# Layer 3 of a four-layer kernel in one pass: each weight part serves both pairs of batches, two block products are added up in PSUM, GpSimd's subtractions go to VectorE

## The chip, the core and the metric

The kernel runs on one core of a Trainium2 chip. The metric is device time in microseconds (us) from launch to end, as the median of several runs; one further execution was profiled. In the profile PE is TensorE's matmul row and PEld its weight loads, DVE is VectorE, ACT ScalarE, POOL GpSimd and SP SyncE, which here issues nearly all DMAs.

## The reference, cut to what matters

```python
scores = cap * tanh((q @ k.T / sqrt(64)) / cap)          # 4 batches, 12 heads, 448 x 64
x   = softmax(scores) @ v                                 # -> 1792 tokens x 768
h   = max(x @ w1, x @ w2, x @ w3)                         # layer 1, 768 x 768 each
y   = h @ w_out                                           # layer 2, 768 x 768
u   = sigmoid(y @ w_gate) * (y @ w_val)                   # layer 3, 768 x 1536 each
out = u @ moe2_w_out                                      # layer 4, 1536 x 768
```

The weights come as 64-bit floats; an fp32 copy is decoded on the chip.

## The kernel before, in words

Every product in fp32 is made of three matmul passes: each operand is split into a high part (an fp32r copy, on ACT) and a low part (operand minus high part), and high·high, high·low and low·high are added up in PSUM. A matmul takes 128 x 128 weights and 448 columns (one batch's tokens).

The stages follow each other in one program: attention and layer 1 are interleaved up to about 400 us; then the rest of layer 1, layer 2, layer 3 and layer 4. The order in which the instructions of one engine stand is made by a scheduler from the order of the code; each engine then works strictly in that order.

**Weights.** `raw_bits` (L51) loads 64-bit words by DMA into a buffer called `wraw`, `decode` (L57) turns them into fp32 with one ACT and four DVE instructions, and `decode_ahead` (L71) does this for the weights of later layers and stores the result in DRAM (`ws`), from where the layers load them again. It is stepped from the loops of layers 1 to 3.

**Layer 3** works with two batches and two column blocks at a time as a 2 x 2 block product in seven products instead of eight (the form of Strassen and Winograd). The text calls one such group a *quad*: column block pair j (0 to 5), gate (m = 0) or value (m = 1) weights, and one pair of batches. Its products are numbered 1, 2, 6, 7, 5, 4, 3; each is nine matmuls. Per quad, `Layer3.prepare` (L425) makes four sums of weight blocks on DVE (L434 to L437) and then, for each product, one weight *part*: a high copy on ACT (L444) and a low one by a subtraction (L445), which for products 1, 2, 4, 7 and 3 is on POOL and for 5 and 6 on DVE. The parts lie in a *ring* of nine slots; the code works four parts ahead (`AHEAD = 4`).

`after` (L468) adds the products up in SBUF (`temps`), seven DVE additions per quad, each with one operand in PSUM. For gate quads a sigmoid on ACT follows (L494), for value quads a multiplication with the gate (L496) and a DMA of the result to DRAM (`us`, L497).

There are two *passes*: 12 quads with the pair of batches (1, 2), then 12 with the pair (3, 0), each loading, summing and splitting all weights anew. So layer 3 has 24 quads, 168 products and 1512 matmuls. The input parts of the second pair are made inside layer 3 by hooks: `build` (L820) splits three chunks each, and five of these seven builds stand in the last quad of the first pass (`half`, L833).

**Layer 4** (L499) is of the same seven-product kind. `form` (L514) makes its weight sums in layer 3's second pass; `first_side` (L527) gives its first weights the `wraw` and `wf` buffers, 1 quad before the end; `fetch` (L509) loads the layer 3 results, `split` (L554) splits them.

Of the kernel before, what the change touches and what calls it, by code (L numbers as in the profile page):

```python
# [17 lines left out]
def tile_kernel(ctx: ExitStack, tc: tile.TileContext, q, k, v, cap, w1, w2, w3, wo, wg, wv, wo2, out):  # L18
# [31 lines left out]

    def raw_bits(wpool, src, shape):  # L51
        raw = wpool.tile([*shape, 2], I32, tag="wraw", name="wraw", bufs=2)
# [14 lines left out]
    def widths(wpool, src, shape):  # L67
        raw = raw_bits(wpool, src, shape)
        return decode(wpool.tile(shape, F32, tag="wf", name="wf", bufs=2), raw)

    def decode_ahead(wpool, items, place):  # L71

        raw, done = None, None
        for src, shape, keep in (*items, (None,) * 3, (None,) * 3):
# [4 lines left out]
            if raw is not None:  # L79
                if place[0] == "s":  # L80
                    t = wpool.tile([P, 3, HC, P], F32, tag="s", name="wd", bufs=1)
                    t = t.rearrange("p a c f -> p (a c f)")[:, :DM]
                else:
                    t = wpool.tile([P, DM], F32, tag="wf", name="wd", bufs=2)
                if len(raw[1]) == 3:
                    t = t.rearrange("p (c f) -> p c f", c=KC)
                done = decode(t, raw[0]), raw[2]
# [10 lines left out]
    def col_block(wpool, w, j, keep=None, kept=False, sub=None):  # L98
        shape = [P, KC, P]
        if kept:  # L100
            wf = wpool.tile(shape, F32, tag="wf", name="wf", bufs=2)
# [285 lines left out]
    def layer2_plain(h2, y2, mm, wpool):  # L387
        wt = col_block(wpool, wo, 0, wso[0], True)
        for j in range(KC):
            this = wt  # L390
            if j + 1 < KC:
                wt = col_block(wpool, wo, j + 1, wso[j + 1], True)
            for h, y in zip(h2, y2):
                ps = mm.tile([P, 512], F32, tag="mm", name="mm")
                product(ps[:, :S], this, h)
                nc.scalar.copy(y[:, j], ps[:, :S])
            yield

    class Layer3:

        AHEAD = 4

        def __init__(self, passes, rooms, mm, wpool, hooks):
            self.passes, self.rooms, self.mm, self.wpool, self.hooks = passes, rooms, mm, wpool, hooks
            self.quads = [(n, j, m) for n in range(len(passes)) for j in range(NF // 2) for m in range(2)]
            self.seq = [(k, i) for k in range(len(self.quads)) for i in (1, 2, 6, 7, 5, 4, 3)]
            self.ready, self.wf, self.sums, self.parts = 0, {}, {}, {}

        def start(self, ring):
            self.ring = [self.rooms.flat(n, "ring") for n in ring]
            self.load(0)
            self.prepare()

        def load(self, k):
            if k < len(self.quads):
                n, j, m = self.quads[k]
# [6 lines left out]
        def prepare(self, upto=AHEAD):  # L425

            while self.ready < min(upto, len(self.seq)):
# [13 lines left out]
                r = self.ready % 9  # L441
                w = self.ring[r // 3][:, (r % 3) * 2 * HC * P : (r % 3 + 1) * 2 * HC * P]
                w = w.rearrange("p (a c f) -> p a c f", a=2, c=HC)
                nc.scalar.copy(w[:, 0], src)  # L444
                (nc.gpsimd if i in (1, 2, 4, 7, 3) else nc.vector).tensor_sub(w[:, 1], src, f(w[:, 0]))  # L445
# [3 lines left out]
        def run(self, temps):  # L449
            self.temps = temps  # L450
            for n, (k, i) in enumerate(self.seq):
                self.prepare(n + 1 + self.AHEAD)
                ps = self.mm.tile([P, 512], F32, tag="mm", name="mm")[:, :S]
                w, x = self.parts.pop((k, i)), self.passes[self.quads[k][0]][1][i]
                order = [(0, m, c) for c in range(HC) for m in range(2)] + [(1, 0, c) for c in range(HC)]
                for q, (wm, xm, c) in enumerate(order):
                    nc.tensor.matmul(  # L457
                        ps, w[:, wm, c, :], x[:, xm, c, :], start=(q == 0), stop=(q == len(order) - 1)
                    )
                self.after(k, i, ps)  # L460
# [3 lines left out]
        def temp(self, k, i):  # L464
            n = (4 * k + i) % 12
            return self.temps[n // KC][:, n % KC]

        def after(self, k, i, ps):  # L468
            c11, c12, c21, c22 = (self.temp(k, e) for e in range(4))
            add = nc.vector.tensor_add  # L470
            if i == 1:
                nc.scalar.copy(c12, ps)
            elif i == 2:
                add(c11, ps, c12)  # L474
                self.out(k, 0, c11)
            elif i == 6:
                add(c12, ps, c12)
            elif i == 7:
                add(c21, ps, c12)
            elif i == 5:  # L480
                add(c12, ps, c12)
                add(c22, ps, c21)
                self.out(k, 3, c22)
            elif i == 4:
                add(c21, ps, c21)
                self.out(k, 2, c21)
            elif i == 3:
                add(c12, ps, c12)
                self.out(k, 1, c12)

        def out(self, k, i, t):
            n, j, m = self.quads[k]
            if m == 0:
                nc.scalar.activation(t, t, AF.Sigmoid)  # L494
            else:
                nc.vector.tensor_mul(t, t, self.temp(k - 1, i))  # L496
                nc.sync.dma_start(out=us[self.passes[n][0][i % 2], 2 * j + i // 2], in_=t)  # L497

    class Layer4:  # L499
# [3 lines left out]
        FORMED = {6: 1, 7: 2, 5: 0, 4: 3}  # L503
# [10 lines left out]
        def form(self, c):  # L514
# [417 lines left out]
```

## Time and profile before

| | us |
|---|---|
| median of three runs | 1060.69 (1057.83 to 1065.54) |
| the profiled execution | 1060.79 |
| its span, first to last instruction | 1059.0 |
| PE busy, sum over the span | 1019.8 |
| DVE busy | 813.5 |
| POOL busy | 188.3 |

PE's row is nearly full over the whole span, because matmuls overlap in it; whether PE loses time is seen where it sat idle and in how many matmuls a stretch holds. DVE, ACT and POOL matter where PE waits for them.

### The profile page before, as it was taken

To read this page: it belongs to the slowest core of one execution; us is meant where nothing else is said; L and a number is where in the kernel's file an instruction comes from. 1 tells how busy PE (TensorE), PEld (TensorE's weight loads), DVE (VectorE), ACT (ScalarE), POOL (GpSimd) and SP (SyncE) were. 2 spreads that over 40 slices of the span, in tenths; PEclk is the share of its full clock that TensorE was granted. 3 is DMA by queue.
4 is the path that set the end of the run, shared out by engine and by line. 5 is a ranking of instruction groups with operands and counts; after the bars stand their busy time and mean duration, and the time that the engine had idled before them with its cause. 6 is when DMAs were issued, how large, how long until landed. Compare 5 with 4: busy or idle time off the path is not lost. (4 is left out here: it accounts for less than half of the span.)

```text
span 1059.0 us, 14671 instructions
## 1 busy us (share of the span) xinstructions
PE 1019.8 (96%) x5197; PEld 848.5 (80%) x5197; DVE 813.5 (77%) x1198; ACT 532.3 (50%) x795; POOL 188.3 (18%) x167
## 2 busy tenths in 40 slices
PE   8989999999999999999999999999699999999997
PEld 4436776777676768999998987788599999999997
DVE  4888699878788786774318999998989866995651
ACT  6886577675775754444435433435434333523230
POOL 1000000000000000004524544353444441000000
PEclk9999999999999999999999999999899999999999
DMA  6767467665665448775126347656874324631232
GB/s 181 259 212 249 139 205 242 223 207 174 224 197 172 150 165 313 243 249 195 59 75 224 109 168 242 205 179 215 277 253 152 118 70 144 211 98 45 83 105 63
DMA packets 95074, 187.84 MB, mean 177 GB/s; under 512 B 33424, under 2 KB 60944, under 8 KB 94480
## 3 DMA queue, kind: packets, MB, share of 16 engines
q1 hardware_dynamic: 94560, 186.48, 53.2%
q8 instruction: 43, 0.70, 0.3%
q10 hardware_dynamic: 432, 0.33, 0.1%
q14 instruction: 39, 0.32, 0.1%
HBM read 139.20 MB, written 47.58 MB: 176 GB/s over the span
## 5 line engine op out<-in xcount | busy, mean ns | idle before, releaser
L457 PE MATMUL mm<-part,ring 128*128 128x448 f32 x1512 | 314.8, 369 | 18.0 <-DVE ring L445 8.6
L457 PEld LDWEIGHTS mm<-part,ring 128*128 128x128 f32 x1512 | 283.3, 189 | 49.3 <-issue 9.6
L141 PE MATMUL mm<-x,wh 128*128 128x448 f32 x864 | 191.9, 371 | 2.6 <-ACT hm L342 1.2
L141 PEld LDWEIGHTS mm<-x,wh 128*128 128x128 f32 x864 | 159.7, 188 | 30.1 <-issue 5.9
L445 POOL TENSOR_TENSOR ring<-w,ring 128x384 fp32r<-128x384 f32 x96 | 120.6, 1264 | 167.6 <-ACT ring L444 144.0
L94 ACT CAST wh<-wf 128x768 fp32r<-128x768 f32 x84 | 69.9, 832 | 102.4 <-DMA wf<-ws 68.6
L95 POOL TENSOR_TENSOR wl<-wf,wh 128x768 fp32r<-128x768 f32 x12 | 23.1, 1923 | 513.4 <-ACT wh L94 493.3
L141 PE MATMUL mm<-x,wl 128*128 128x448 f32 x432 | 100.8, 369 | 0.6 <-DVE wl L95 0.5
L268 ACT ACTIVATE e<-e,capb 128x896 f32<-128x896 f32 (+1 forms) x96 | 88.9, 948 | 1.0
L141 PEld LDWEIGHTS mm<-x,wl 128*128 128x128 f32 x432 | 80.4, 188 | 9.8 <-DVE wl L95 3.0
L574 PE MATMUL mm<-w2a,u 128*128 128x384 f32 x504 | 88.0, 334 | 0.0
L574 PEld LDWEIGHTS mm<-w2a,u 128*128 128x128 f32 x504 | 87.4, 188 | 0.0
L95 DVE TENSOR_TENSOR wl<-wf,wh 128x768 fp32r<-128x768 f32 x72 | 68.6, 953 | 12.0 <-ACT wh L94 11.5
L260 ACT ACTIVATE e<-sc,tsc 128x896 f32<-128x896 f32 (+1 forms) x78 | 73.9, 968 | 4.4 <-PE sc L255 4.4
L494 ACT ACTIVATE temps<-temps 128x448 f32<-128x448 f32 x48 | 27.8, 580 | 80.5 <-DVE temps L474 32.3
L574 PE MATMUL mm<-w2b,u 128*128 128x384 f32 x378 | 66.0, 334 | 0.0
L574 PEld LDWEIGHTS mm<-w2b,u 128*128 128x128 f32 x378 | 65.6, 188 | 0.0
L288 PE MATMUL pv<-e,vs 128*64 128x448 f32 x288 | 61.3, 548 | 3.1 <-DVE r L308 3.1
L141 PE MATMUL mm<-h,wh 128*128 128x448 f32 x288 | 63.4, 369 | 0.0
L444 ACT CAST ring<-s 128x384 fp32r<-128x384 f32 x72 | 36.6, 508 | 52.5 <-DVE s L435 33.2
L444 ACT CAST ring<-w 128x384 fp32r<-128x384 f32 x96 | 48.1, 510 | 28.3 <-PE mm L457 18.9
L558 ACT CAST u<-u 128x1344 fp32r<-128x1344 f32 x24 | 31.6, 1322 | 57.9 <-PE mm L574 53.8
(136 smaller groups left out, 1448.8 us busy)
## 6 DMA issues: line engine op xcount, KB each, us to landing
wf<-ws SPq DMA_DIRECT2D x64, 384.0 KB, 3.7
w<-ws SPq DMA_DIRECT2D x48, 384.0 KB, 3.4
wraw<-in_moe_w_dram SPq DMA_DIRECT2D x18, 768.0 KB, 4.8
wraw<-in_moe_w_out_dram SPq DMA_DIRECT2D x18, 768.0 KB, 5.3
ws<-wd SPq DMA_DIRECT2D x36, 384.0 KB, 2.7
us<-temps SPq DMA_DIRECT2D x48, 224.0 KB, 2.0
u<-us SPq DMA_DIRECT2D x8, 1344.0 KB, 7.4
wraw<-in_moe_w_gate_dram SPq DMA_DIRECT2D x12, 768.0 KB, 5.6
```

The costliest lines, as they stand in the source:

```text
L94: nc.scalar.copy(wh, wf)
L95: (sub or nc.gpsimd.tensor_sub)(wl, wf, f(wh))
L141: nc.tensor.matmul(ps, a[:, c, :], at(x, m, c), start=(n == 0), stop=(n == len(passes) - 1))
L260: nc.scalar.activation(e, sc[:, :w, :S], AF.Tanh, scale=tsc)
L268: nc.scalar.activation(e, e, AF.Exp, scale=1.0 if self.general else capb)
L288: nc.tensor.matmul(self.pv[0][own, :S], lhs, e, start=(c == 0), stop=(c is None))
L444: nc.scalar.copy(w[:, 0], src)
L445: (nc.gpsimd if i in (1, 2, 4, 7, 3) else nc.vector).tensor_sub(w[:, 1], src, f(w[:, 0]))
L457: nc.tensor.matmul(ps, w[:, wm, c, :], x[:, xm, c, :], start=(q == 0), stop=(q == len(order) - 1))
L494: nc.scalar.activation(t, t, AF.Sigmoid)
L558: nc.scalar.copy(high, src[:, own])
L574: nc.tensor.matmul(ps, a, ww[g][:, w], start=(c == 0 and m == 0), stop=(c == KC - 1 and m == 2))
```

## The change

It is in layer 3 and around it.

- There is one pass. Quads are (j, m) with a list of pairs: j = 5 for the first pair (two quads), then j = 0 to 4 for both pairs (ten quads), then j = 5 for the second pair (two). Each weight part serves the first pair's product and then the second's. Parts to make: 14 quads x 7 = 98, before 168; matmuls: 1512 as before.
- The products come in the order 1, 6, 7, 2, 5, 4, 3. Product 2 is added onto product 1's bank in PSUM and product 3 onto product 5's, so five additions per quad and pair remain of seven.
- All the low parts are made on DVE; POOL has nothing to do in layer 3. The ring has three slots in the `wraw` and `wf` buffers, and `AHEAD` is 2.
- Layer 2 for the second pair (`layer2_second`) makes parts 1, 2 and 5 of that pair at once; parts 6, 7, 3 and 4 are built in the two first quads.
- All gate and value weights are decoded before layer 3 (one item every second step of layer 1's rest, before every third). Layer 4's weights are decoded and summed in layer 3 by `last_weights`, through a single `wraw` buffer, in place.
- `first_side` takes the ring's third slot for the last third of layer 4's first low weights, in the last quad, after product 5.

```diff
-    def layer2_plain(h2, y2, mm, wpool):
+    def layer2_second(h2, parts, y3, y0, t2, mm, wpool):
...
+            pa, pb = (mm.tile([P, 512], F32, tag="mm", name="mm")[:, :S] for _ in range(2))
+            product(pa, this, h2[0])
+            split(parts[1 if j < HC else 2], c, pa)
+            product(pb, this, h2[1])
+            if j < HC:
+                nc.scalar.copy(y0[:, j], pb)
+                nc.vector.tensor_sub(y3[:, j], y0[:, j], pa)
+                split(parts[5], c, y3[:, j])
...
     class Layer3:
-        AHEAD = 4
+        AHEAD = 2
+        ORDER = (1, 6, 7, 2, 5, 4, 3)
+        ONTO = {2: 1, 3: 5}
...
+            end = NF // 2 - 1
+            self.quads = [(end, m, (0,)) for m in range(2)]
+            self.quads += [(j, m, (0, 1)) for j in range(end) for m in range(2)]
+            self.quads += [(end, m, (1,)) for m in range(2)]
...
+            raw = one_of(self.wpool, "wraw", 1, [P, 2 * size], F32R, "ring")
+            self.ring = [raw[:, :size], raw[:, size:], one_of(self.wpool, "wf", 1, [P, size], F32R, "ring")]
...
                 nc.scalar.copy(w[:, 0], src)
-                (nc.gpsimd if i in (1, 2, 4, 7, 3) else nc.vector).tensor_sub(w[:, 1], src, f(w[:, 0]))
+                nc.vector.tensor_sub(w[:, 1], src, f(w[:, 0]))
...
+                for p in self.quads[k][2]:
+                    onto = self.ONTO.get(i)
+                    if onto:
+                        ps = self.open.pop((p, onto))
+                    else:
+                        ps = self.mm.tile([P, 512], F32, tag="mm", name="mm")[:, :S]
+                    if i in self.ONTO.values():
+                        self.open[p, i] = ps
...
         def first_side(self):
+            raw = one_of(self.wpool, "wraw", 0, [P, 2 * DM], F32R, "w2a")
+            high = [block(raw[:, :DM]), block(raw[:, DM:]), block(one_of(self.wpool, "wf", 0, [P, DM], F32R, "w2a"))]
+            low = [block(self.wpool.tile([P, DM], F32R, tag=tag, name="w2a", bufs=2)) for tag in ("wh", "wl")]
+            self.sides[0] = [high, low + [block(one_of(self.wpool, "wf", 1, [P, DM], F32R, "w2a"))]]
...
-            for j in range(NF):
+            for j in (*range(NF - 2, NF), *range(NF - 2)):
                 later_weights += [(cols(w, j), [P, KC, P], ws3[m, j]) for m, w in enumerate((wg, wv))]
-            later_weights += [(wo2[j * P : (j + 1) * P, :], [P, DM], ws2[j]) for j in range(NF)]
...
-            if i % 3 == 0:
+            if i % 2 == 0:
                 next(ahead)
...
+        def last_weights():
+            for c in range(KC):
+                for r in (c, KC + c):
+                    raw = raw_bits(wpool, wo2[r * P : (r + 1) * P, :], [P, DM])
+                    yield
+                    wf = decode(two(wpool, "wf", [P, DM], F32, "wd"), raw)
+                    nc.sync.dma_start(out=ws2[r], in_=wf)
+                    yield
+                t = l4.load_sums(c)
+                yield
+                l4.form(c, t)
+                yield
...
+            ((0, 1), lambda: build(6, t2, 8)),
+            ((0, 5), lambda: build(7, y0[:, tops], 9)),
+            ((1, 1), lambda: build(3, y0[:, ends], 7)),
+            ((1, 5), lambda: [build(4, y3[:, ends], 1), l3.free.extend(temps(0))]),
+            *(((k, i), step) for k in range(2, end - 1) for i in (1, 7, 5, 3)),
...
+            ((end, 7), lambda: l4.fetch("11", 1, 8)),
+            ((end, 2), lambda: l4.fetch("21", 1, 9)),
+            ((end, 5), lambda: [l4.first_side(), l4.weights(0)]),
```

How the scheduler orders it follows in rows of the built programs: line, operation, result<-operands, size, and how often in a row. The lines of the changed kernel have other numbers: `ring` L465 was L445, the sums L456 to L459 were L434 to L437, the additions are L506 to L520, the layer 3 matmuls L485, those of layer 4 L618.

First place: DVE in the middle of layer 3 while weights of layer 4 are decoded (`wd`). Before, a stretch of the first pass:

```order
L474 TENSOR_TENSOR temps<-mm,temps 128x448
L61 TENSOR_SCALAR wd<-wd 128x768
L62 TENSOR_SCALAR wd<-wd 128x768
L63 SCALAR_TENSOR_TENSOR wd<-wraw,wd 128x768
L477 TENSOR_TENSOR temps<-mm,temps 128x448
L445 TENSOR_TENSOR ring<-s,ring 128x384
L479 TENSOR_TENSOR temps<-mm,temps 128x448
L64 SCALAR_TENSOR_TENSOR wd<-wraw,wd 128x768
```

Now, in a quad that serves both pairs:

```order
L465 TENSOR_TENSOR ring<-s,ring 128x384
L456 TENSOR_TENSOR s<-w_5428 128x384
L457 TENSOR_TENSOR s<-s,w_5426 128x384
L458 TENSOR_TENSOR w_5428<-w_5426,w_5428 128x384
L514 TENSOR_TENSOR temps<-mm,temps 128x448
L459 TENSOR_TENSOR s<-w_5426,s 128x384
L72 TENSOR_SCALAR wd<-wd 128x768
L514 TENSOR_TENSOR temps<-mm,temps 128x448
L465 TENSOR_TENSOR ring<-w_5426,ring 128x384
L73 TENSOR_SCALAR wd<-wd 128x768
```

The ring's subtractions of the blocks `w` now stand on DVE between the two pairs' additions (L514 twice) and the decoding; before, they stood on POOL. POOL's own list has no L465.

Second place: SP's list in the same part of layer 3. Before:

```order
L497 DMA us<-temps 128x448 x3
L422 DMA w_5617<-ws_58 128x768
L76 DMA ws_61<-wd 128x768
L54 DMA wraw<-in_moe_w_out_dram 128x1536
L422 DMA w_5619<-ws_58 128x768
L422 DMA w_5736<-ws_58 128x768
```

Now:

```order
L65 DMA wraw<-in_moe2_w_out_dram 128x1536
L444 DMA w_6010<-ws_58 128x768
L884 DMA ws_61<-wd 128x768
L556 DMA formed<-ws_61 128x768 x2
L565 DMA wt_62<-formed 128x1536
L65 DMA wraw<-in_moe2_w_out_dram 128x1536
L444 DMA w_6209<-ws_58 128x768
```

The load of a raw slice (`wraw`) now stands right behind the store of the weight sums (`wt`) that leaves the same buffer, and the weight loads of the next quad (`w`) stand behind it.

Third place: TensorE at the hand-over from layer 3 to layer 4. Before:

```order
L141 MATMUL mm<-h,wh 128x448 x12
L141 MATMUL mm<-h,wl 128x448 x6
L457 MATMUL mm<-part,ring 128x448 x1512
L574 MATMUL mm<-w2a,u_7930 128x384 x2
L574 MATMUL mm<-w2a,u_7931 128x384
```

Now:

```order
L147 MATMUL mm<-h,wl 128x448 x6
L485 MATMUL mm<-part,ring 128x448 x1503
L618 MATMUL mm<-w2a,u_7503 128x384
L485 MATMUL mm<-part,ring 128x448 x9
L618 MATMUL mm<-w2a,u_7503 128x384
L618 MATMUL mm<-w2a,u_7504 128x384
```

And DVE's list there, now (`w2a` is layer 4's first weights, its last row the third of them that uses the ring's slot):

```order
L531 TENSOR_TENSOR temps<-mm,temps 128x448
L465 TENSOR_TENSOR ring<-s,ring 128x384
L608 TENSOR_TENSOR u<-u 128x1344
L514 TENSOR_TENSOR temps<-mm,temps 128x448
L608 TENSOR_TENSOR u<-u 128x1344
L531 TENSOR_TENSOR temps<-temps 128x448
L517 TENSOR_TENSOR temps<-mm,temps 128x448
L520 TENSOR_TENSOR temps<-mm,temps 128x448
L531 TENSOR_TENSOR temps<-temps 128x448 x2
L603 TENSOR_TENSOR u_7504<-u,u_7503 128x3x448
L603 TENSOR_TENSOR u_7579<-u,u_7578 128x3x448
L593 TENSOR_TENSOR w2a<-w2a 128x768
```

One matmul of layer 4 now stands ahead of layer 3's last product; and DVE reaches the last third of layer 4's first low weights behind eleven other rows, among them the two splits of `u` (L603).

## Rows read from the trace of the kernel before

**Rows 1.** The page: busy time of each engine, and the span in 40 slices.
```profile
PE 1019.8 (96%) x5197; PEld 848.5 (80%) x5197; DVE 813.5 (77%) x1198; ACT 532.3 (50%) x795; POOL 188.3 (18%) x167
...
DVE  4888699878788786774318999998989866995651
```

**Rows 2.** The chain that ended last: start us, us, what.
```profile
752.72 146.61 PE mm L457 x714
899.33 152.90 PE mm L574 x882
```

**Rows 3.** Stretches of layer 3: busy time of each engine, clock, DMA.
```profile
core 0: us, PE busy (x) PEld busy (x) DVE busy (x) ACT busy (x) POOL busy (x), PEclk, DMA share, GB/s
...
581.50:619.80 38.30, 38.30 (x191) 35.54 (x190) 38.30 (x57) 17.13 (x35) 21.45 (x16) 1.00 0.36 119
619.80:734.10 114.30, 107.19 (x505) 92.81 (x504) 107.31 (x166) 41.53 (x86) 50.00 (x40) 1.00 0.60 201
734.10:758.70 24.60, 15.27 (x64) 12.98 (x63) 24.60 (x38) 13.14 (x29) 11.86 (x9) 0.79 0.79 257
758.70:899.20 140.50, 140.50 (x695) 130.31 (x695) 114.06 (x180) 55.19 (x108) 55.93 (x50) 1.00 0.47 159
```

**Rows 4.** Groups, 566 to 900 us: busy us, mean ns | idle before, releasers.
```profile
L457 PE MATMUL mm<-part,ring 128*128 128x448 f32 x1512 | 314.8, 369 | 18.0 <-DVE ring L445 8.6 <-DVE temps L479 3.1 <-DVE temps L477 2.1
...
L445 POOL TENSOR_TENSOR ring<-w,ring 128x384 fp32r<-128x384 f32 x96 | 120.6, 1264 | 167.6 <-ACT ring L444 144.0 <-PE mm L457 21.2 <-DVE ring L445 2.4
...
L445 DVE TENSOR_TENSOR ring<-s,ring 128x384 fp32r<-128x384 f32 x48 | 37.0, 775 | 3.8 <-ACT ring L444 3.8
...
L474 DVE TENSOR_TENSOR temps<-mm,temps 128x448 f32<-128x448 f32 x24 | 14.7, 614 | 5.4 <-PE mm L457 4.3 <-ACT ring L444 1.0
...
L64 DVE SCALAR_TENSOR_TENSOR wd<-wraw,wd 128x768 int32<-128x768 int32 x11 | 13.7, 1247 | 0.0
...
L62 DVE TENSOR_SCALAR wd<-wd 128x768 int32<-128x768 int32 x10 | 6.0, 613 | 0.1
...
L559 DVE TENSOR_TENSOR u<-u,u 128x1344 fp32r<-128x1344 f32 x2 | 3.1, 1548 | 0.0
L549 DVE TENSOR_TENSOR w2a<-w2a 128x768 fp32r<-128x768 f32 x3 | 2.8, 948 | 1.2 <-ACT w2a L548 1.2
```

**Rows 5.** PE in order of time at the end of layer 2.
```profile
562.85 2.64 PE L141 MATMUL mm<-h,wh 128*128 128x448 f32 x12
565.33 1.40 PE L141 MATMUL mm<-h,wl 128*128 128x448 f32 x6
```

**Rows 6.** In order of time: DVE and POOL at the end of the first pass.
```profile
743.07 3.79 DVE L132 TENSOR_TENSOR part<-y,part 128x448 fp32r<-128x448 f32 x3
743.65 2.73 POOL L445 TENSOR_TENSOR ring<-w,ring 128x384 fp32r<-128x384 f32 x2
...
752.12 0.54 DVE L445 TENSOR_TENSOR ring<-s,ring 128x384 fp32r<-128x384 f32 x1
```

**Rows 7.** A stretch behind the longest wait of PE, columns as in rows 3.
```profile
752.70:756.30 3.60, 3.58 (x10) 3.20 (x11) 3.60 (x7) 2.45 (x5) 1.52 (x2) 0.50 0.94 350
```

**Rows 8.** DMAs by kind: issues, KB each, median us to landing.
```profile
wraw<-in_moe_w_out_dram SPq DMA_DIRECT2D x18, 768.0 KB, 5.3
...
us<-temps SPq DMA_DIRECT2D x48, 224.0 KB, 2.0
u<-us SPq DMA_DIRECT2D x8, 1344.0 KB, 7.4
...
wt<-formed SPq DMA_DIRECT2D x6, 768.0 KB, 4.9
...
w2a<-ws SPq DMA_DIRECT2D x6, 384.0 KB, 3.9
```

**Rows 9.** A stretch of layer 1's rest, columns as in rows 3.
```profile
400.00:425.00 25.00, 25.00 (x121) 22.45 (x120) 17.75 (x28) 9.18 (x13) 0.00 (x0) 1.00 0.85 310
```

**Rows 10.** In order of time: a wait of PE's weight loads there (in brackets).
```profile
421.39 2.36 PEld L141 LDWEIGHTS mm<-x,wh 128*128 128x128 f32 x12 [0.34 <-ACT wh L94]
```

More of the change, by code (lines that the diff above doesn't have):

```diff
@@ L48, in f, with one_of, two @@
         return ap.bitcast(F32)
+    turn, single = {}, [False]
+    def one_of(wpool, tag, n, shape, dt, name):
+        return wpool.tile(shape, dt, tag=f"{tag}{n}", name=name, bufs=1)
+    def two(wpool, tag, shape, dt, name):
+        n = 0
+        if not single[0]:
+            n = turn[tag] = 1 - turn.get(tag, 1)
+        return one_of(wpool, tag, n, shape, dt, name)
     def raw_bits(wpool, src, shape):
-        raw = wpool.tile([*shape, 2], I32, tag="wraw", name="wraw", bufs=2)
+        raw = two(wpool, "wraw", [*shape, 2], I32, "wraw")
         dims = "p c f t -> p c (f t)" if len(shape) == 3 else "p f t -> p (f t)"
@@ L446, in prepare, with run @@
                 self.parts[k, i] = w
                 self.ready += 1
-        def run(self, temps):
-            self.temps = temps
+        def run(self, free):
+            self.free = free
+            order = [(0, m, c) for c in range(HC) for m in range(2)] + [(1, 0, c) for c in range(HC)]
             for n, (k, i) in enumerate(self.seq):
                 self.prepare(n + 1 + self.AHEAD)
[L453 to L460, printed above, removed]
+                w = self.parts.pop((k, i))
+                for p in self.quads[k][2]:
+                    onto = self.ONTO.get(i)
+                    if onto:
+                        ps = self.open.pop((p, onto))
+                    else:
+                        ps = self.mm.tile([P, 512], F32, tag="mm", name="mm")[:, :S]
+                    if i in self.ONTO.values():
+                        self.open[p, i] = ps
+                    x = self.xs[p][i]
+                    for q, (wm, xm, c) in enumerate(order):
+                        nc.tensor.matmul(
+                            ps,
+                            w[:, wm, c, :],
+                            x[:, xm, c, :],
+                            start=(q == 0 and not onto),
+                            stop=(q == len(order) - 1),
+                            skip_group_check=bool(onto),
+                        )
+                    self.after(k, p, i, ps)
@@ L461, in run, with new @@
                 for hook in self.hooks.get((k, i), ()):
                     hook()
[L464 to L470, printed above, removed]
-            if i == 1:
-                nc.scalar.copy(c12, ps)
-            elif i == 2:
[L474 to L479, printed above, removed]
+        def new(self):
+            return self.free.pop(0)
```

206 lines of the change are left out of this document (101 added, 105 removed).

## The prediction

> **What bounds the kernel now.** The page comes first: PE is busy for 1019.8 us of 1059.0, DVE for 813.5, and DVE's digits stand at 8 and 9 through the stretch in which POOL works [rows 1]. The chain of waits says where PE bounds without help: from 752.72 us to the end it is matmuls of layer 3 and of layer 4 and nothing else [rows 2]. Nothing is to be had there but by a faster matmul; what can be had lies before it.
>
> The stretches of layer 3 give the floor. Quads 1 to 3 take 38.30 us (191 matmuls are counted, of which two reach in from outside; three quads have 189), so 202.65 ns each, with DVE just as full, 38.30 of 38.30 [rows 3]. At that pace 1512 matmuls take 306.4 us. Layer 3 begins where layer 2's last six matmuls end: twelve take 565.33 − 562.85 = 2.48 us, 206.7 ns each, so six more end at 566.57 [rows 5]. It ends at 899.33 [rows 2]. That is 332.76 us for 306.41: **26.3 us are lost**. By stretch, each against 63 matmuls a quad at 202.65 ns:
> quad 0 takes 14.9 for 12.8 (2.2 lost); quads 4 to 11 take 114.30 for 102.1 (12.1); quad 12, in the stretch from 734.10, 24.60 for 12.8 (11.8); the second pass, eleven quads, 140.6 for 140.4 (0.2) [rows 3]. Of it, PE's idle time is 18.0 us, put down to DVE's ring subtractions (8.6) and to additions that free PSUM banks [rows 4]. The rest is slower matmuls around the stops; one part is plain, 3.60 us with ten matmuls at a granted clock of 0.50, the lower level of 1.2 GHz, behind the longest stop: 1.8 us [rows 7].
>
> So DVE sets the time in quads 0, 4 to 11 and 12. What ails it there is seen in rows of one shape. A ring subtraction takes 775 ns in the mean, one that stands alone 540; three L132 take 3.79 us while two subtractions run on POOL; an addition with one operand in PSUM keeps its 614 [rows 4, 6]. DVE operations with two inputs in SBUF stretch beside POOL.
>
> **The change, part by part.** *DVE's load.* Ring subtractions on DVE go from 48 to 98, sums from 96 to 56, additions from 168 to 120; 24 operations form layer 4's sums and 48 multiplications stay. With POOL idle I take the short duration: (98 + 56 + 24) × 0.540 = 96.1; (120 + 48) × 0.614 = 103.2; twelve decodings at the durations beside POOL, 2 × (1.247 + 0.613) = 3.72 each, 44.6, their upper end; twelve subtractions of builds at 3.79 / 3, 15.2, also upper; layer 4's first operations 3.1 + 2.8 [rows 4, 6]. Together 265 us of 306, 86%. Before, DVE was busy for 284.3 of the 317.7 us from 581.50, 89%, and in quads 4 to 11 for 107.31 of 114.30 [rows 3]. POOL's 96 subtractions of plain blocks alone took 120.6 us at 1264 ns [rows 4]; a part whose low half came from there was late by more than one on DVE is.
>
> The Trainium skill speaks against this part: Perfetto Trace Analysis, Optimizing Scalar/DVE Operations, says that handing work of a saturated DVE to GpSimd may make sense, though the two share a read port of SBUF and it might not help. The change does the reverse, on the engine that was full. The stretched rows agree with the port; whether taking the work back costs more than the port did is what the first rival is about.
>
> *What is removed.* The losses of quads 4 to 12, 23.9 us, and quad 0's 2.2 lie on the path. Quad 12's five builds in one quad become four, in two quads at the start; the rest moves to layer 2. I remove all 26.3 and set new terms.
>
> *Pace.* Matmuls stood at 202.65 ns in layer 3 and at 206.7 in layer 2 [rows 3, 5]. Nothing here tells which one the new layer 3 gets. Bounds 0 and 1512 × 4.05 ns = 6.1; I take **3.0**.
>
> *New waits in layer 3.* Parts are now two ahead instead of four, but a part serves two products: 2 × 2 × 9 × 0.20265 = 7.3 us, as long as four products were. In this time DVE has at worst a decoding (3.7), four additions or multiplications (2.5) and the part's subtraction (0.5): 6.7. It fits by 0.6. In the four single quads the time is 3.65, and a build (3 × 0.61), the four sums (2.2) and the subtraction make 4.5: late by up to 0.9, four times at most. For bounds: quads 1 to 3, with DVE full and no decoding in them, lost nothing; quads 4 to 11, with DVE full and eleven decodings, lost 12.1, 1.1 a decoding, which is 13.2 for twelve [rows 3, 4]. DVE is less full than in either, so I take **3.5**, a quarter.
>
> *Loads.* The weight loads go from 48 to 28; those of 384 KB, and the 48 result stores that stay, take 2 to 4 us each [rows 8]. One raw buffer now takes every raw slice (5.3) and every store of sums (4.9) in turn; it lies off the path as long as the decoding that DVE has in its row finds its data. The third rival prices it.
>
> *Rest of layer 1.* A decoding every second step instead of every third. One stretch there has a DMA share of 0.85 at 310 GB/s, DVE at 17.75 of 25 [rows 9], and PE's weight loads waited 0.34 us once [rows 10]. A few more such waits: ten would be 3.4. The stretch's 121 matmuls in 25 us are the slow pace; some 800 matmuls to layer 3's start at the fast one would give back 3.3. Bounds −3.3 and 3.4; I take **1.0**, as DMA is nearer to full than PE to a change of pace. Layer 2's second half gets 21 subtractions on DVE, 13 us at 0.614, in six steps of 7.4 us (36 matmuls at 206.7 ns): two steps in seven, and I cost them at nothing; if DVE is held up by decodings there, the banks come free later and the price is a few waits as in the row above.
>
> *Hand-over.* Layer 4's first product takes its weights in the order of thirds, so after layer 3's product 5 of the last quad there stand 18 matmuls of layer 3 and 36 of layer 4 ahead of the third low part: 18 × 0.2027 + 36 × 152.90 / 882 = 9.9 us [rows 2, 3]. It needs its load (3.9, up to 7.4 behind the two fetches of u), a copy on ACT of about 1, and 0.948 on DVE [rows 4, 8]: 5.8 to 9.4. Ahead of it on DVE stand eleven rows, two of them 1.55 us, so that it may be late by up to 4.5, if the load comes late and they don't overlap. Bounds 0 and 4.5; I take **1.0**. The first weights' high thirds have other buffers and come earlier.
>
> Sum: 1060.8 − 26.3 + 3.0 + 3.5 + 1.0 + 1.0 = **1043.0 us**. The profiled execution's 1060.79 is 0.1 from the median, so no correction is made.
>
> **The rivals.** *First: DVE stays the bound.* If the operations don't shrink without POOL (something else in this stretch, DMA writes or ACT, stretches them), 178 × 0.775 = 138 replaces 96.1 and DVE's load is 307 us, 100% of PE's time. In quads 4 to 11 a full DVE was busy for 94% of the time: 307 / 0.94 = 326.6, so 20.2 us lost instead of 3.5, **1059.7**. For it: DVE full in all of quads 0 to 12, and the ring of three instead of nine. Against it: the 540 ns beside the 775. The Trainium skill's port rule (same section) is against it, its advice to unload a saturated DVE for it.
>
> *Second: the hand-over stalls.* DVE serves the splits first, PE stops for 4.5, and the clock falls to 0.50 as it did behind the longest stop (1.8) [rows 7]: 1043.0 + 3.5 + 1.8 = **1048.3**. For it: the order on DVE. Against: the load can be issued as soon as product 5 has left the slot.
>
> *Third, on the slower side: the single raw buffer.* A decoding stands in DVE's row four operations or two products behind the issue of its load. If that is too short, DVE waits in its row, with the ring's subtractions and the additions queued behind it, and PE behind these. Load and decoding take 5.3 + 3.7 = 9.0 against 7.3: 1.7 late, twelve times; six times the load stands behind a store of 4.9 on the same buffer. 20.4 + 29.4 = 49.8 instead of 3.5: **1089**. It decides from the point at which a raw load lands after DVE has reached its decoding. For it: the two SP rows that follow each other. Against: the steps are a quad's quarters apart, and on the two-pair quads a quarter is 6.4 us, so that load and store have a step each.
>
> **How the numbers follow.** Forecast 0.68; first rival 0.14; second 0.10; third 0.04; all new terms at their good ends (1043.0 − 3.0 − 3.5 − 1.0 − 4.3 = 1031) 0.04. The range leaves out the third and the first: low **1034**, where the pace and the waits cost nothing and the hand-over 1.0; high **1056**, the forecast with new waits at 13.2 and the hand-over at 4.5 (1056.2). A measurement of this kernel tells about 1% (10.6 us) from no change: faster is below 1050.1, slower above 1071.3. Faster: 0.04 + 0.10 and 0.64 of the forecast's 0.68 (the rest has several waits at once), **0.78**. Within 1%: 0.14 and that rest, **0.18**. Slower: **0.04**.
>
> **What would show it.** POOL's digits at 0 from layer 3 on; DVE's ring group at about 540 ns (775 would be the first rival); windows from 567 to about 880 us with idle time of PE at some 3 us, in the first two quads and around decodings; the pace at 202.65 or 206.7; no stretch at clock 0.50 in the middle; at the end of layer 3 a wait for `w2a` of 1 us or less (4 and a half clock: second rival). PE idle put down to a decoding with DVE idle for `wraw` before it is the third. The prediction is wrong above all if layer 1's rest or layer 2 runs into DMA, for which only one stretch and one wait stand here.

## The result and the profile after

| | before | changed |
|---|---|---|
| median, runs side by side | 1061.28 us (4 runs) | 1031.55 us (1030.15 to 1033.78, 4 runs) |
| the profiled execution | 1060.79 | 1033.78 |
| its span | 1059.0 | 1031.9 |

The ratio is 0.972, with a 95% interval of 0.968 to 0.976. The change makes the kernel 2.8% faster, more than was forecast: the measured time lies 2.5 us under the low end of the range.

The page of the changed kernel, as [rows 1]:

```profile
PE 1011.9 (98%) x5197; PEld 849.1 (82%) x5197; DVE 751.2 (73%) x1164; ACT 505.7 (49%) x719; POOL 39.1 (4%) x47
...
DVE  4889699887878878676526967777766479976561
...
POOL 1000000000000000002541000000000000000000
```

POOL does nothing from layer 3 on, and DVE's digits in the middle of layer 3 have come down from 9 to 7; at both its ends they stay at 9. The end of the chain of waits (start us, us, what) stands for [rows 2]:

```profile
398.14 167.40 PE mm L147 x810
565.54 305.11 PE mm L485 x1503
870.82 1.82 PE mm L485 x9
872.64 152.75 PE mm L618 x881
```

Matmuls alone, without a stop, from 398 us to the end. Layer 3 runs from 565.54 to 872.64: 307.1 us for 332.6 between the same marks before, where its matmuls at the fast pace need 306.4. (Read from the first matmul's start, it runs from 565.38 to 872.48, and before from 566.57 to 899.16.) Its stretches, as [rows 3]: the two first quads (one pair each), the ten with both pairs, the two last.

```profile
core 0: us, PE busy (x) PEld busy (x) DVE busy (x) ACT busy (x) POOL busy (x), PEclk, DMA share, GB/s
565.50:591.50 26.00, 26.00 (x128) 23.53 (x127) 25.67 (x52) 15.41 (x31) 0.00 (x0) 1.00 0.40 135
591.50:846.80 255.30, 255.30 (x1262) 236.57 (x1261) 175.95 (x313) 79.58 (x143) 0.00 (x0) 1.00 0.45 155
846.80:872.60 25.80, 25.80 (x129) 23.93 (x128) 24.03 (x37) 12.73 (x22) 0.00 (x0) 1.00 0.81 275
```

DVE is busy for 225.7 us of 307.1, 73%, very unevenly: 69% in the ten quads, 99% in the first two. PE waits in neither. The groups of layer 3, as [rows 4], show no idle time ahead of the matmuls, and short durations for DVE's rows that read SBUF twice; the addition with one operand in PSUM (L506) is as it was:

```profile
L485 PE MATMUL mm<-part,ring 128*128 128x448 f32 x1510 | 306.9, 365 | 0.0
...
L465 DVE TENSOR_TENSOR ring<-w,ring 128x384 fp32r<-128x384 f32 x55 | 30.4, 553 | 13.2 <-PE mm L485 10.2 <-ACT ring L464 3.0
...
L465 DVE TENSOR_TENSOR ring<-s,ring 128x384 fp32r<-128x384 f32 x42 | 23.1, 551 | 7.2 <-PE mm L485 7.0 <-ACT ring L464 0.2
...
L506 DVE TENSOR_TENSOR temps<-mm,temps 128x448 f32<-128x448 f32 x24 | 15.0, 624 | 19.8 <-PE mm L485 19.7
...
L75 DVE SCALAR_TENSOR_TENSOR wd<-wraw,wd 128x768 int32<-128x768 int32 x10 | 9.5, 954 | 0.1
```

The ring's subtraction of the sums takes 551 ns (775 before), the decoding's last operation 954 (1247 before). Ten decodings stand in layer 3.

### The profile page after: what moved, and what is told of

Its sections match the earlier page's. It is cut to its first block, busy times and chain, and to the rows that moved or that the text cites. A ratio compares the mean times of both kernels' runs of the same rounds, so it can differ in the third digit from the quotient of the medians.

```text
span 1031.9 us, 14092 instructions
## 1 busy us (share of the span) xinstructions
PE 1011.9 (98%) x5197; PEld 849.1 (82%) x5197; DVE 751.2 (73%) x1164; ACT 505.7 (49%) x719; POOL 39.1 (4%) x47
## 4 chain that ended last, share of the span: by engine, by line
PE 69%; DVE 12%; ACT 11%; DMA 4%; issue 4%; ACTq 0%; DVEq 0%; SPq 0%
PE mm L485 30%; PE mm L147 19%; PE mm L618 15%; ACT e L266 4%; ACT e L274 3%; DMA wf<-ws 2%; PE pv L294 2%; DVE wl L101 1%; DMA wraw<-in_moe_w_dram 1%; DVE sum L284 1%; ACT wh L100 1%; PE sc L261 1%; DVE xn L320 1%; DVE xn L321 1%; PE pv L306 1%
## 5 line engine op out<-in xcount | busy, mean ns | idle before, releaser
L485 PE MATMUL mm<-part,ring 128*128 128x448 f32 x1512 | 307.3, 365 | 0.0
L485 PEld LDWEIGHTS mm<-part,ring 128*128 128x128 f32 x1512 | 283.8, 188 | 23.1
L618 PE MATMUL mm<-w2a,u 128*128 128x384 f32 x504 | 88.2, 334 | 0.0
L618 PEld LDWEIGHTS mm<-w2a,u 128*128 128x128 f32 x504 | 87.4, 188 | 0.1
L101 DVE TENSOR_TENSOR wl<-wf,wh 128x768 fp32r<-128x768 f32 x72 | 68.6, 953 | 11.5 <-ACT wh L100 10.2
L618 PE MATMUL mm<-w2b,u 128*128 128x384 f32 x378 | 66.0, 334 | 0.0
L618 PEld LDWEIGHTS mm<-w2b,u 128*128 128x128 f32 x378 | 65.6, 188 | 0.0
L464 ACT CAST ring<-w 128x384 fp32r<-128x384 f32 x56 | 28.6, 511 | 69.7 <-PE mm L485 60.5
L147 PEld LDWEIGHTS mm<-h,wh 128*128 128x128 f32 x288 | 54.1, 188 | 5.5
L71 ACT ACTIVATE wd<-wraw 128x768 f32<-128x768 f32 x42 | 38.1, 908 | 35.7 <-DMA wraw<-in_moe_w_out_dram 13.7
L464 ACT CAST ring<-s 128x384 fp32r<-128x384 f32 x42 | 21.5, 512 | 62.8 <-PE mm L485 51.9
L603 DVE TENSOR_TENSOR u<-u,u 128x1344 fp32r<-128x1344 f32 x24 | 37.1, 1554 | 16.6 <-ACT u L602 16.6
```

The source lines that it names most:

```text
L71: nc.scalar.activation(wf, high.bitcast(F32), AF.Abs)
L101: (sub or nc.gpsimd.tensor_sub)(wl, wf, f(wh))
L147: nc.tensor.matmul(ps, a[:, c, :], at(x, m, c), start=(n == 0), stop=(n == len(passes) - 1))
L485: nc.tensor.matmul(ps, w[:, wm, c, :], x[:, xm, c, :], start=(q == 0 and not onto), stop=(q == len(order) - 1), skip_group_check=bool(onto),)
L603: nc.vector.tensor_sub(self.part[h][1][:, :, cols], src[:, own], f(high))
L618: nc.tensor.matmul(ps, a, ww[g][:, w], start=(c == 0 and m == 0), stop=(c == KC - 1 and m == 2))
```

## The experiments

The theory that they set out from, **slack**: in the changed kernel every weight part is ready 2 to 8 us before its use, because a part serves two products and DVE has time left, so that no single edit matters. Its rivals: **the port** (what matters is that POOL no longer stretches DVE's operations), **the load** of DVE, as the prediction had it, and **the ring** of three. Ratios are against the kernel before on the same chip, with the 95% interval; the experiments stand on three chips.

**The changed kernel again.**

> The changed kernel once more, to stand beside its variants on the same chip. Both theories: 1030 to 1034 us. Its trace also tells whether the few us between its runs come from the pace of the matmuls ahead of layer 3: if so, a span that is some 3.5 us shorter has 202.65 ns instead of 206.7 from about 410 to 590 us (880 matmuls x 4.05 ns = 3.6 us), and layer 3 is no different.

1032.27 us, 0.974 (0.971 to 0.978). Its profiled execution, 1033.41, again has the slow pace ahead of layer 3 (810 matmuls in 167.5 us), so it doesn't show the other case; the next run but one does.

**POOL's part undone** (in the changed kernel):

```diff
-                nc.vector.tensor_sub(w[:, 1], src, f(w[:, 0]))
+                (nc.gpsimd if i in (1, 2, 4, 7, 3) else nc.vector).tensor_sub(w[:, 1], src, f(w[:, 0]))
```

> 70 of the 98 low parts back on POOL (products 1, 2, 4, 7 and 3, as before). Theory of slack (in the changed kernel each weight part is ready 2 to 8 us before its use, so that one edit undone costs nothing): DVE loses 70 x 0.47 = 33 us of work, its operations with two inputs in SBUF stretch beside POOL, PE waits 0 to 2 us in layer 3, 1031 to 1034 us. Theory of the port (the waits went because POOL no longer disturbs DVE): the ring's subtractions on DVE go back from 0.55 to 0.7 or more and PE's waits come back by about 10 us, 1041 us or more.

1041.99 us, 0.982 (0.980 to 0.985). Slack is wrong on the size: ten us come back. The port isn't right either in the way it was put: the ring's DVE rows go to 581 ns only, and the ten quads with both pairs lose 0.7 us, at their start. Of 7.2 us lost in layer 3, 6.5 are lost in the single-pair quads, most of it in one stop. PE, in order of time, waits in brackets; then DVE ahead of the stop:

```profile
569.84 7.81 PE L485 MATMUL mm<-part,ring 128*128 128x448 f32 x37
580.87 3.36 PE L485 MATMUL mm<-part,ring 128*128 128x448 f32 x11 [3.23 <-DVE temps L514]
```

```profile
573.64 2.78 DVE L138 TENSOR_TENSOR part<-y,part 128x448 fp32r<-128x448 f32 x2
...
576.88 1.44 DVE L138 TENSOR_TENSOR part<-y,part 128x448 fp32r<-128x448 f32 x2
...
580.11 0.61 DVE L514 TENSOR_TENSOR temps<-mm,temps 128x448 f32<-128x448 f32 x1
```

L514 is the addition that reads product 5's bank. Product 3 is to be added onto that bank and can't begin before L514 has read it: the open bank is a wait that no kernel without adding up in PSUM has. L514 is queued behind builds, two of which take 2.78 us beside POOL. The four builds ahead of it take 4.1 us from start to start, where four at the undisturbed 0.53 would take 2.1. That is about 2 of the 3.2; DVE's order is another here as well (sums and a row of layer 4's weights stand ahead of L514), since the scheduler sets it anew with each edit, and how much of the rest is due to that is not separated. Five matmuls behind the stop, nine take 373 ns each: the granted clock is 0.50 there, the lower level.

**Adding up in PSUM undone** (in the changed kernel):

```diff
-        ORDER = (1, 6, 7, 2, 5, 4, 3)
-        ONTO = {2: 1, 3: 5}
+        ORDER = (1, 2, 6, 7, 5, 4, 3)
+        ONTO = {}
```

and the two additions per quad and pair that this asks for. The order of the products changes with it, here and in the other runs on this part of the change, so the two are not told apart.

> The two block products that are added up in PSUM are added in SBUF again, 48 more additions on DVE, 25 us at a spacing of 0.53, products in the old order. Theory of slack: DVE goes from about 73% to 81% of layer 3, PE waits 0 to 2 us, 1031 to 1034 us. Theory that DVE's load is what counts (86% was costed at 3.5 us in the prediction): 2 to 4 us more, 1034 to 1036 us.

1032.04 us, 0.974 (0.970 to 0.979): nothing, as slack has it. The profiled execution took 1029.24 us, and its chain tells most of why that is 4.5 us under the changed kernel's:

```profile
396.83 164.36 PE mm L147 x810
561.19 306.43 PE mm L485 x1512
867.62 153.09 PE mm L621 x882
```

The 810 matmuls ahead of layer 3 take 164.36 us here and 167.40 in the changed kernel's profile: 202.9 ns each and 206.7, or 3.0 us. Layer 3 is at 202.65 throughout.

**DVE's work doubled and more** (in the changed kernel, the line of the low part written three times, then five times):

> Each low part of the ring is computed three times over, the same values; 196 more subtractions on DVE, 92 us at a spacing of 0.47. DVE's load in layer 3 goes from 223 us to 315, over the 306 that PE needs. Theory that DVE's load was the bound of the kernel before: PE's waits come back, layer 3 takes at least 315 us and some 330, 1040 to 1056 us, with PE's waits put down to DVE. Theory that load is not what counts but the port: no more than the 9 us by which 315 is over 306, 1040 us.

> Each low part is computed five times, 392 more subtractions on DVE. The run with three showed the ten quads of both pairs at 252 us for 232 us of DVE work (92%) without a wait. Theory of a threshold (DVE costs nothing up to its full time, then what it is over): in the ten quads DVE has 176 + 4 x 70 x 0.47 = 308 us of work for 255, so they take about 308, 53 us more. Theory that losses grow with load from far below (as the prediction had it): at 92% there would have been some already. Whole: layer 3 some 380 us, 1105 us.

Three times: 1051.64 us, 0.992 (0.989 to 0.994), and layer 3 takes 329.5 us: the time is the one of the first theory, and over the second's 1040. Stretches of that run, the middle one from a third of the way into the third quad to just behind the twelfth:

```profile
563.00:608.00 45.00, 39.80 (x173) 33.86 (x171) 44.11 (x91) 18.55 (x37) 0.00 (x0) 0.92 0.24 81
608.00:860.00 252.00, 251.90 (x1233) 230.97 (x1231) 232.45 (x447) 78.17 (x140) 0.00 (x0) 1.00 0.47 160
860.00:893.00 33.00, 26.93 (x120) 22.95 (x119) 30.76 (x58) 12.46 (x20) 0.00 (x0) 0.95 0.64 222
```

With DVE busy for 232.45 of 252 us, 92%, PE is busy for 251.90. So where DVE keeps up, a load of 92% costs next to nothing. Of the 23.1 us that layer 3 loses against 306.4, 15.9 are in the four single-pair quads, where DVE had next to no time to spare in the changed kernel, and 4.8 in the third quad, which follows the first two. Five times: 1120.68 us in one run, and in the ten quads DVE is over its full time:

```profile
606.40:907.10 300.70, 270.13 (x1258) 236.75 (x1258) 297.52 (x598) 76.21 (x141) 0.00 (x0) 0.98 0.39 134
```

They take 300.7 us, DVE's 297.5 and little more (308 was expected; layer 3 as a whole takes 396.6 for 380, as the two ends lost more). So in a long stretch load cost nothing at 92%, and in this one run about what it was over where it was beyond 100% (45 us more for 42 of excess). This decides against a price that grows with the load.

**A ring of two** (in the changed kernel):

```diff
-        AHEAD = 2
+        AHEAD = 1
...
-            self.ring = [raw[:, :size], raw[:, size:], one_of(self.wpool, "wf", 1, [P, size], F32R, "ring")]
+            self.ring = [raw[:, :size], raw[:, size:]]
+            one_of(self.wpool, "wf", 1, [P, size], F32R, "ring")
```

The third slot's buffer stays reserved and unused.

> The ring has two slots instead of three and parts are made one product ahead instead of two. In the changed kernel's trace a low part is ready 5.3 to 7.7 us before its use in the ten quads with both pairs and 2.2 to 5 us in the four with one; one product less takes 3.65 and 1.82 us of that. Theory of slack: no wait in the ten, 0 to 5 us in the four single ones, layer 3 307 to 312 us, 1031 to 1037 us. First rival of the prediction (the short ring is what binds): some 20 us of waits, spread over all quads, 1050 us.

1034.54 us, 0.974 (0.970 to 0.977). Layer 3 takes 308.7 us: three waits of 0.2 to 0.4 us in single-pair quads, none in the ten. The ring of three has slack, and the first rival's ring part falls.

**The kernel before with POOL idle:**

```diff
-                (nc.gpsimd if i in (1, 2, 4, 7, 3) else nc.vector).tensor_sub(w[:, 1], src, f(w[:, 0]))
+                nc.vector.tensor_sub(w[:, 1], src, f(w[:, 0]))
```

> The kernel before with all ring subtractions on DVE; POOL idle in layer 3. Theory that POOL's help and its disturbance cancel: 120 x 0.47 = 56 us more on DVE, against some 40 us of stretching that goes (48 ring subtractions x 0.23, sums, multiplications, decodings, builds), within 8 us of the kernel before, 1052 to 1068 us; quads 4 to 11 have 14.1 us of DVE work each for 12.8 of PE and stay bound by DVE. Theory that DVE's number of operations alone counts: 56 us more on a full engine, 1085 us or more.

1043.9 us, 0.984 (0.981 to 0.988). Neither expectation held: 120 operations more on the engine that was full, and the kernel is 17 us faster. Stretches: quads 0 to 11, quad 12, the rest of the second pass; then the group.

```profile
563.50:716.70 153.20, 153.20 (x758) 142.00 (x757) 151.27 (x287) 76.54 (x153) 0.00 (x0) 1.00 0.51 167
716.70:738.00 21.30, 15.75 (x65) 13.69 (x64) 21.30 (x42) 5.94 (x12) 0.00 (x0) 0.84 0.82 287
738.00:881.00 143.00, 143.00 (x694) 129.91 (x693) 131.47 (x250) 56.84 (x112) 0.00 (x0) 1.00 0.57 192
```

```profile
L445 DVE TENSOR_TENSOR ring<-w,ring 128x384 fp32r<-128x384 f32 x96 | 52.3, 551 | 1.1 <-ACT ring L444 0.8
```

The 12 quads that lost 14.3 us [rows 3] lose none, with DVE busy for 151.27 of 153.20. What was a full and late engine beside POOL is a full and timely one alone. This is what the port's theory says of POOL, on the kernel where DVE had no time to spare: the run shows that DVE's rows are stretched beside POOL and not without it (551 ns); that a port is the reason, no run shows. A loss at quad 12 stays, 8.5 us of 11.8.

**The kernel before with adding up in PSUM** (the order 1, 6, 7, 2, 5, 4, 3, products 2 and 3 on the banks of 1 and 5, two additions fewer per quad):

```diff
-            self.seq = [(k, i) for k in range(len(self.quads)) for i in (1, 2, 6, 7, 5, 4, 3)]
+            self.seq = [(k, i) for k in range(len(self.quads)) for i in (1, 6, 7, 2, 5, 4, 3)]
...
-                ps = self.mm.tile([P, 512], F32, tag="mm", name="mm")[:, :S]
+                onto = {2: 1, 3: 5}.get(i)
+                if onto:
+                    ps = self.open.pop(onto)
+                else:
+                    ps = self.mm.tile([P, 512], F32, tag="mm", name="mm")[:, :S]
+                if i in (1, 5):
+                    self.open[i] = ps
...
```

> The kernel before with one part of the change: two block products added up in PSUM, products in the new order, 48 additions fewer on DVE. Theory of a threshold: quads 4 to 11 lost 12.1 us with DVE over its full time; without 16 additions (8.5 us) DVE comes to about 99 of 102 us there and most of the loss goes; quad 12 keeps its five builds and loses some 10. Layer 3 320 to 325 us, 1048 to 1053 us. Theory that the parts, not the additions, are what PE waits for: within 3 us of the kernel before.

1070.65 us, 1.010 (1.006 to 1.013): 1% slower, with 48 operations fewer on the engine that bounds. The group of its layer 3 matmuls, with idle time and releasers; then PE in order of time, from the first wait for L491 on:

```profile
L463 PE MATMUL mm<-part,ring 128*128 128x448 f32 x1511 | 321.5, 375 | 24.1 <-DVE temps L491 20.5 <-ACT ring L444 2.9 <-DVE ring L445 0.7
```

```profile
582.25 14.60 PE L463 MATMUL mm<-part,ring 128*128 128x448 f32 x63 [2.73 <-DVE temps L491]
597.56 13.03 PE L463 MATMUL mm<-part,ring 128*128 128x448 f32 x63 [0.71 <-DVE temps L491]
612.68 27.36 PE L463 MATMUL mm<-part,ring 128*128 128x448 f32 x126 [2.08 <-DVE temps L491]
```

L491 is the addition that reads product 5's bank, as L514 above. There are ten such waits; those shown stand 63 matmuls apart, one quad, each ahead of product 3, with product 4's nine matmuls behind product 5. Those nine take 1.8 us and L491 0.6, so L491 may begin some 1.2 us late. In the ten quads that wait it begins 1.6 to 7.2 us after product 4's first matmul, in the fourteen others at most 0.6. Both expectations were wrong, for the same reason: the open bank had no place in them.

**Both in the kernel before** (POOL idle and adding up in PSUM, the two edits above):

> The kernel before with both parts: all low parts on DVE, and two products added up in PSUM. Each alone gave 1043.9 and 1070.7 us (1061 before). Theory of the open bank (adding up in PSUM cost 9 us because an addition queued behind stretched work on DVE holds the bank that product 3 needs one product later): with DVE unstretched the waits go, quads 0 to 11 lose nothing, quad 12's builds lose 8 as without it, 1040 to 1046 us. Theory that the open banks cost by themselves (a product less between an addition and its user): some 9 us over the kernel with DVE alone, 1053 us.

1035.27 us, 0.978 (0.976 to 0.981), below both ranges. PE in order of time, layer 3 and the first of layer 4:

```profile
561.52 1.99 PE L463 MATMUL mm<-part,ring 128*128 128x448 f32 x9
564.74 306.22 PE L463 MATMUL mm<-part,ring 128*128 128x448 f32 x1503 [1.23 <-ACT ring L444]
870.80 19.43 PE L584 MATMUL mm<-w2a,u 128*128 128x384 f32 x111
```

The waits for the open bank go, as its theory has it: L491 now begins at most 1.4 us after product 4's first matmul in 23 quads (3.0 in the other, where five more matmuls stand in between), PE's waits for it are 0.2 us or less, and layer 3 takes 309.3 us. PE waits once for longer than half a microsecond, at the start. That quad 12 with its five builds loses nothing either, at 202.7 ns a matmul, was in neither expectation; 24 additions fewer stand on DVE ahead of it, but why it goes is not shown. Two passes, with all 168 parts made, come within 0.4% of the changed kernel.

**Both undone in the changed kernel:**

> The changed kernel with both undone: 70 low parts on POOL, and no adding up in PSUM. With POOL alone undone it took 1042.0 us, and PE's one long stop (3.2 us at 577) was for the addition that reads product 5's open bank, which product 3 has to add onto. Theory of the open bank: without open banks that stop goes, layer 3 307 to 310 us, 1031 to 1036 us, although DVE has 48 more additions. Theory of the port and of load: more work on DVE beside the same POOL work, 1042 us or more.

1039.21 us, 0.981 (0.979 to 0.983). Layer 3 takes 309.1 us, as the open bank's theory has it: the stop at 577 us is gone. But the median is 3 us over what it allows. In the profiled execution (1037.34 us) layer 4 waits at its start:

```profile
872.28 6.61 PE L621 MATMUL mm<-w2a,u 128*128 128x384 f32 x37
879.79 2.20 PE L621 MATMUL mm<-w2a,u 128*128 128x384 f32 x11 [0.90 <-ACT w2a L595]
884.00 2.18 PE L621 MATMUL mm<-w2a,u 128*128 128x384 f32 x11 [2.01 <-DVE w2a L596]
```

That is the second rival of the prediction, at 2.9 us and without its lower clock. The first of the two waits is for the copy on ACT, which stands behind the load; the second is for DVE. In the changed kernel both are missed by little (below).

**The kernel before with POOL idle and light builds** (ACT copies the low parts of the five builds in quad 12, so their values are not the reference's):

```diff
-                split(later[i], c, src[c] if isinstance(src, list) else src[:, c])
+                t = src[c] if isinstance(src, list) else src[:, c]
+                if i in (6, 7, 5, 4, 3):
+                    nc.scalar.copy(later[i][:, 0, c, :], t)
+                    nc.scalar.copy(later[i][:, 1, c, :], t)
...
```

> The kernel before with all low parts of the ring on DVE, and the five builds in quad 12 without DVE: their low parts are copied by ACT instead of subtracted (not the reference's values). Theory that the builds are the rest of what the change gained: quad 12's loss of 8.4 us falls to 0 to 2 and the half clock behind it goes, 1034 to 1038 us, within 4 us of the changed kernel, without one pass. Theory that the loss there comes from the change of passes (new weights, no parts of the next quad ready): it stays within 3 us, 1041 us or more.

1037.67 us, 0.980 (0.976 to 0.984). Quad 12's loss falls from 8.5 us to 1.8, of it one wait of 1.5, without the half clock: it is the builds' DVE work. The time is in the first theory's range, but not within 4 us of the changed kernel: in the profiled execution the 774 matmuls of layer 3 ahead of that wait have the slow pace of 206.7 ns, 3.0 us.

**Decoding in every step of layer 1's rest** (in the changed kernel):

```diff
-            if i % 2 == 0:
-                next(ahead)
+            next(ahead, None)
...
```

> The changed kernel with a decoding in every step of layer 1's rest instead of every second, until the weights are done. DVE there has about 10 us of its own work and 6.7 x 3.0 = 20 us of decoding per 25 us, 120%; DMA some 25% more than at its share of 0.86. Theory of a threshold: some 12 steps from 400 us on over the full time by 0.75 us each: 5 to 15 us, 1037 to 1047 us, with PE waiting for the split weights in layer 1. Theory that this stage has room left: 1030 to 1034 us.

1032.64 us, 0.975 (0.972 to 0.979). It doesn't test what it was made for: the edit moved hardly any decoding. The group of their first operation from 398 to 473 us, in this run:

```profile
L71 ACT ACTIVATE wd<-wraw 128x768 f32<-128x768 f32 x8 | 7.3, 906 | 6.0 <-DMA ws<-wd 5.9
```

Eight begin in these 75 us, as in the changed kernel, seven of them within 1.1 us of the same times (the second at 421.51 and 421.50), the last 3.4 us earlier. The code's step number doesn't set their pace. Four of the eight wait on ACT for the store of the decoding before (`ws<-wd`), which leaves the one buffer that they all use; what holds the others, and how much room the stage has, stays open. In this execution the pace ahead of layer 3 is the fast one (810 matmuls in 164.5 us), and layer 3 takes 307.4 us, with one wait of 0.4 us for L514, the open bank.

## Why the prediction was wrong

The direction held, and so did the mechanism of what is removed: DVE's rows are short without POOL, and PE's waits go. What failed is the size of the new terms, the one for new waits in layer 3 above all: the time was 11.5 us too high and outside the range. Term by term, in the profiled execution:

- **What is removed, −26.3:** right. PE's 18.0 us of idle time in layer 3 are 0.0, the half clock is gone, and layer 3 is 25.5 us shorter, 0.5 of the loss being left as pace. The prediction's 332.76 runs from a start to an end mark that lies 0.17 later; between like marks it is 332.59, and the term −26.2.
- **Pace, 3.0:** measured 0.5. Only the two first quads have 206.7 ns, 126 × 4.05 ns. The value was half of a two-way case.
- **New waits in layer 3, 3.5:** measured 0.0. This is the largest step that failed, in two ways. First, DVE's load was put at 265 us by count times duration; it is 226. Twelve decodings were counted and ten stand in layer 3, decodings and builds were costed as stretched, and the durations overlap: in the run with POOL idle the rows of additions start 0.53 us apart and show 0.61 to 0.62 each. Second, a quarter of "1.1 a decoding" was taken from quads 4 to 11, where DVE was over its full time (107.31 us of work for 102.1 of matmuls [rows 3]). The eleven decodings are those of all of layer 3: of their last operations eight start in quads 4 to 11 and two in quads 1 to 3 (at 607.1 and 619.7), which the prediction took to have none and which lost nothing. The trace had the answer: a decoding cost nothing where DVE kept up. The run with three subtractions shows next to no wait at 92%, the kernel before without POOL none at 99%.
- **Rest of layer 1, 1.0:** measured −1.2: layer 3's first matmul starts at 565.38 instead of 566.57, and the 0.34 us wait [rows 10] is not there. The step behind the term was wrong: "a decoding every second step instead of every third" is what the code says, but 15 decodings stand between 398 us and layer 3 in both traces; what paces them is shown only in part (above).
- **Hand-over, 1.0:** measured 0, by half a microsecond and less. DVE at the end of layer 3, and its last third of the first low weights:

```profile
874.29 3.02 DVE L603 TENSOR_TENSOR u<-u,u 128x1344 fp32r<-128x1344 f32 x2
877.23 0.95 DVE L593 TENSOR_TENSOR w2a<-w2a 128x768 fp32r<-128x768 f32 x1
```

It ends at 878.18, and the matmul that needs it, the 38th of layer 4, starts at 878.75. The account of it (5.8 to 9.4 for 9.9) was right; so was the row of splits in front. What the prediction had wrong is that the high thirds come earlier: the last one is copied by ACT from the same load, ends at 876.12, and its first user, the 24th matmul, starts at 876.30. That margin is the smaller one.

With these the sum is 1060.8 − 26.2 + 0.5 − 1.2 = 1033.9, against 1033.78. The median is 2.2 us lower. Both profiled executions of the changed kernel have the slow pace ahead of layer 3; other kernels have the fast one in theirs, as the run without adding up in PSUM and the one with a decoding in every step (layer 3 began at 561.0 and 562.0 us). That the faster executions of the changed kernel have it too is likely and not shown. The bounds of that pace were in the prediction, −3.3, but the value was put on the other side.

The low end of the range does not follow from what was named for it: with pace and waits at nothing, 1.0 for layer 1 and 1.0 for the hand-over, the sum is 1036.5. Its 1034 is about what is left with every new term at nothing, 1034.5, and the profiled execution is there. All good ends together were 1031, and that case, given a chance of 0.04, is the one that the median shows. So of the miss of 11.5 us some 9 are in the four terms; by how much the median fell below the range hangs on the pace, which is chance.

The first rival fell at its condition: the operations did shrink (553 ns). The Trainium skill's two sentences (Perfetto Trace Analysis, Optimizing Scalar/DVE Operations) can now be weighed on a run. On this kernel its warning that offloading to GpSimd might not help held, and not its advice to unload a saturated DVE: taking all of POOL's subtractions back gained 17 us by itself. The rows agree with the shared read port that it gives as the reason, but no run here shows the port itself. The third rival, the single raw buffer, shows nowhere: no wait of PE in the ten quads.

What the prediction didn't have is the open bank, a wait that the change adds. It costs nothing in the changed kernel's profile, where two pairs alternate and DVE is prompt (0.4 us in the run with a decoding in every step), and 20.5 us of PE's idle time in the kernel before beside POOL. And the credit goes elsewhere than the change's name says. Low parts on DVE alone give 17 us, with adding up in PSUM 24; one pass and the builds moved to layer 2 come to some 4 us beyond that, measured on different chips and about what the pace makes between executions.

## What to carry to other kernels

Before work is taken off a full engine, look at what the helper does to it: compare the duration of one row beside the helper and without. An engine that feeds another cost nothing here as long as its work was under the time and each deadline had room for what was queued ahead; price an overload by the excess, measured from start to start of its operations, and not by a share of a loss from a stretch that was over the limit. Adding up in an open PSUM bank made the next product on it wait for the addition that reads it; count what is queued ahead of that reader.

## What the runs showed of the hardware

- Beside POOL, DVE's operations with two inputs in SBUF took longer in the mean and those with one input in PSUM did not: the ring's subtraction 775 ns for 551, a build's 928 for 618, an addition 614 for 620 (the kernel before, with and without POOL).
- The same matmuls ran at 206.7 or 202.65 ns for hundreds in a row at full clock. In the changed kernel the pace changed at 590.8 us, at one matmul that came 16 ns late, without a wait that the trace shows; what decides it stays open. Over the 810 matmuls ahead of layer 3 it is worth 3 us, as much as all that lies between the changed kernel and the best two-pass one.
